# A streaming gate kernel: six fixed slots, a first tile of 8 rows on one queue, and the first loads issued ahead of the opening barrier

## The chip, the cores and the metric

The kernel runs on one core of a Trainium2 chip. The metric is device time in microseconds (us) of that core. Kernels are compared only within the same rounds. Ratios are the mean time of one kernel's fast executions over that of the other's in the same rounds, so they are not quite the ratio of the medians that the text quotes.

## The reference, cut to what matters

```python
# x: (1, 384, 384, 384) bfloat16, w1d: one bfloat16 weight
g = jnp.einsum("bhwc->bc", x) / (H * W)      # mean of each channel over 147,456 pixels
s = sigmoid(g * w1d[0])                      # 384 gates
return x * s[:, None, None, :]               # every pixel times its channel's gate
```

The input has 113.25 MB and so has the output. A gate is known only after all pixels have been summed, so a plain kernel would read the input twice. Both kernels here read it once. They compute an early gate `s_early` from the first tile and multiply and store with it while they sum everything; at the end they compare it with the true gate in bfloat16 and repeat the whole pass only if a bit differs. In these data it never differs, because the gates round to the same value.

## The kernel before

A "row" is 128 pixels (one for each partition, 768 bytes in each). The kernel cuts the 1,152 rows into tiles of 44 (the last two have 28 and 24) and keeps six of them in the on-chip memory. SyncE's queue carries loads and ScalarE's queue carries stores. The first four tiles are loaded half on one queue and half on the other. TensorE sums each tile by 33 matmuls with a matrix of ones, VectorE multiplies it by `s_early` in place, and ScalarE issues the store. The load of tile k waits for the store of tile k-6.

```python
EDGE, SLOT, BOTH = 44, 44, 4

def load(place, n, r0, queues=("sync",)):
    of = dram(x_rows, r0, n)
    i = 0
    for queue, m in zip(queues, split(n, -(-n // len(queues)))):
        plan.dma(queue, at(place + i, m), of[:, i * C : (i + m) * C], writes=rows(place + i, m))
        i += m

def put(place, n, r0, to):                      # gate, then store
    plan.op("vector", gate(to, place, n, s_early), ...)
    plan.final.append(plan.dma("scalar", dram(o_rows, r0, n), at(to, n), reads=rows(to, n)))

for k in range(BOTH):
    load(places[k], sizes[k], starts[k], ("sync", "scalar"))
    if k == 0:
        plan.dma("scalar", w_one[0:1, 0:1], w1d.unsqueeze(0), writes=["w_one"])
heads = {e: len(plan.streams[e]) for e in ("sync", "scalar")}
weight()                                        # the weight, by a small matmul
add_rows(places[0], sizes[0], 0, True, True)    # sum of the first tile, for s_early
# ... s_early ...
for k in range(1, len(sizes)):
    if k >= n_slots:
        j = k - n_slots
        put(places[j], sizes[j], starts[j], places[j])
    if k >= BOTH:
        load(places[k], sizes[k], starts[k])
    add_rows(places[k], sizes[k], 1, k == 1, k == last)   # 33 matmuls, written out
for k in range(len(sizes) - n_slots, last):
    put(places[k], sizes[k], starts[k], places[k])
put(places[last], sizes[last], starts[last], places[last + 1 - n_slots])
# ... true gate, comparison, conditional second pass ...

plan.emit("sync", nc.sync, heads["sync"])       # first loads: after the opening barrier,
plan.emit("scalar", nc.scalar, heads["scalar"]) # before the engines' blocks
```

Of the kernel before, what the change touches and what calls it, by code (L numbers as in the profile page):

```python
# [3 lines left out]
P = 128  # L4
# [9 lines left out]
class Planner:  # L14
# [9 lines left out]
    def __init__(self, nc, name, n_dma_sems):  # L24
        self.nc = nc
        self.streams = {e: [] for e in ("sync", "scalar", "vector", "tensor", "gpsimd")}
        self.sems = {e: nc.alloc_semaphore(f"{name}_{e}") for e in self.COMPUTE}
        self.count = {e: 0 for e in self.COMPUTE}
        self.pool = [nc.alloc_semaphore(f"{name}_dma_{i}") for i in range(n_dma_sems)]
        self.pool_uses = [0] * n_dma_sems  # L30
        self.n_dma = 0
        self.writer = {}
        self.readers = {}
        self.seen = {e: {} for e in self.streams}
        self.final = []

    def _wait(self, engine, token):
        sem, value = token
        if self.seen[engine].get(sem.name, 0) >= value:
            return  # L40
        self.seen[engine][sem.name] = value
        self.streams[engine].append(("wait", sem, value))

    def _needs(self, reads, writes):
# [12 lines left out]
        return list(need.values())  # L57
# [8 lines left out]
    def op(self, engine, emit, reads=(), writes=(), signal=True):  # L66
# [10 lines left out]
        self.streams[engine].append(("op", emit, self.sems[engine] if signal else None, 1))  # L77
        self._record(token, reads, writes)

    def dma(self, engine, out, in_, reads=(), writes=()):  # L80
# [11 lines left out]
        )  # L92
        self._record(token, reads, writes)
        return token

    def emit(self, name, e, most=None):
# [3 lines left out]
        for kind, a, b, *c in now:  # L100
            if kind == "wait":
                e.wait_ge(a, b)
            else:
# [11 lines left out]
EDGE, SLOT, BOTH = 44, 44, 4  # L115


def bass_standalone__channel_attn_eca__vision_kernel(
# [15 lines left out]
    s_true = nc.alloc_sbuf_tensor("s_true", [P, C], BF16)  # L134
    w_one = nc.alloc_sbuf_tensor("w_one", [1, 16], BF16)
    w_scaled = nc.alloc_sbuf_tensor("w_scaled", [P, 2], F32)
    warm = nc.alloc_sbuf_tensor("warm", [P, 2], F32)
# [23 lines left out]
    n_slots = n_arena // SLOT  # L161
    full, rest = divmod(n_rows - EDGE, SLOT)
    if rest < EDGE:
        full, rest = full - 1, rest + SLOT
    sizes = [EDGE] + [SLOT] * full + [4 * q for q in split(rest // 4, EDGE // 4)]
    assert sum(sizes) == n_rows and max(sizes) <= SLOT
    plan = Planner(nc, "a", 50)

    def load(place, n, r0, queues=("sync",)):
        of = dram(x_rows, r0, n)  # L170
        i = 0
        for queue, m in zip(queues, split(n, -(-n // len(queues)))):
# [3 lines left out]
                of[:, i * C : (i + m) * C],  # L176
# [22 lines left out]
    def add_rows(place, n, group, first, last):  # L199

        n_wide = n * C // WIDE
        start = place * C
        for i in range(n_wide):
            bank = acc[group][i % 3]
            plan.op(
                "tensor",
                lambda e, i=i, bank=bank: mm(e,
                    bank[:, :],
                    ones[:],
                    arena[:, start + i * WIDE : start + (i + 1) * WIDE],  # L210
                    start=first and i < 3,
                    stop=last and i >= n_wide - 3,
                ),
                reads=["ones"] + (rows(place, n) if i in (0, n_wide - 1) else []),
                writes=[f"acc{group}"],
                signal=i == n_wide - 1,
            )

# [15 lines left out]
    def put(place, n, r0, to):  # L234
        plan.op(
            "vector",
            gate(to, place, n, s_early),
            reads=["s_early"] + rows(place, n),
            writes=rows(to, n),
        )  # L240
        plan.final.append(
            plan.dma("scalar", dram(o_rows, r0, n), at(to, n), reads=rows(to, n))
        )

    def weight():
# [15 lines left out]
        for i, n in enumerate((sizes[0], n_rows)):  # L261
# [9 lines left out]
    starts = [sum(sizes[:k]) for k in range(len(sizes))]  # L271
    places = [k % n_slots * SLOT for k in range(len(sizes))]
    last = len(sizes) - 1


    plan.op("gpsimd", lambda e: e.memset(warm[:, 0:1], 0.0), writes=["warm"])  # L276
    plan.op("vector", lambda e: e.memset(ones[:], 1.0), writes=["ones"])  # L277
    for k in range(BOTH):
        load(places[k], sizes[k], starts[k], ("sync", "scalar"))
        if k == 0:  # L280
            plan.dma("scalar", w_one[0:1, 0:1], w1d.unsqueeze(0), writes=["w_one"])
    heads = {e: len(plan.streams[e]) for e in ("sync", "scalar")}
    weight()
    add_rows(places[0], sizes[0], 0, True, True)
# [8 lines left out]
    )  # L293



    for k in range(1, len(sizes)):
        if k >= n_slots:
            j = k - n_slots
            put(places[j], sizes[j], starts[j], places[j])  # L300
        if k >= BOTH:
            load(places[k], sizes[k], starts[k])
        add_rows(places[k], sizes[k], 1, k == 1, k == last)
    for k in range(len(sizes) - n_slots, last):
        put(places[k], sizes[k], starts[k], places[k])
    put(places[last], sizes[last], starts[last], places[last + 1 - n_slots])


# [4 lines left out]
            s_true[:], total[:], ACT_F.Sigmoid, scale=w_scaled[:, 1:2]  # L313
        ),
        reads=["total", "w_scaled1"],
        writes=["s_true"],
# [4 lines left out]
            total[:], s_true[:].bitcast(U16), s_early[:].bitcast(U16), ALU.not_equal  # L321
# [19 lines left out]
    again = Planner(nc, "b", 50)  # L341
    for place, n, r0 in zip(places, sizes, starts):
# [3 lines left out]
            gate(place, place, n, s_true),  # L346
            reads=rows(place, n),
# [4 lines left out]
        )  # L352
    for token in again.final:
# [3 lines left out]
    plan.emit("sync", nc.sync, heads["sync"])  # L357
    plan.emit("scalar", nc.scalar, heads["scalar"])
# [68 lines left out]
```

## Time and profile before

| | |
|---|---|
| time, median of 6 | 530.01 us (529.88 to 530.04); 529.97 us when the prediction was made |
| span of the profiled execution | 528.2 us (that execution took 529.65 us) |
| bytes moved, mean rate | 226.57 MB, 429 GB/s |
| TensorE, VectorE busy | 46% each |

These are lines of the page of the kernel before: busy time of each engine, the DMA share (in tenths) and the rate in 40 equal slices of the span, and the DMA queues with packets, MB and share of the 16 DMA engines. Queue 1 is SyncE's, queue 10 ScalarE's, queues 8 and 14 carry instructions.

```profile
span 528.2 us, 1091 instructions
PE 243.4 (46%) x865; PEld 0.2 (0%) x2; DVE 241.2 (46%) x45; ACT 2.7 (1%) x4; POOL 0.3 (0%) x5
...
DMA  8999999999999999999999999999999999999998
GB/s 361 431 426 420 448 415 447 433 427 438 422 448 425 438 433 427 433 426 450 427 433 433 427 448 417 445 427 433 430 429 450 427 433 430 429 429 434 442 427 363
...
q10 hardware_dynamic: 4466, 121.90, 53.6%
q1 hardware_dynamic: 3888, 104.60, 46.1%
q8 instruction: 3, 0.05, 0.0%
q14 instruction: 3, 0.02, 0.0%
```

The DMA engines are busy from end to end; only the first and the last slice are weaker. No compute engine is near its limit. The other view is the timeline of the first microseconds of the kernel before (start, length, engine and instruction; a `q` marks the engine's issue of transfers):

```profile
0.73 0.41 ACTq L91 DMA_DIRECT2D arena<-in_x_dram  x1
...
0.74 2.40 SPq L91 DMA_DIRECT2D arena<-in_x_dram  x5
```

The first loads are issued at 0.73 and 0.74 us. The trace's record of single DMA packets adds that the first packet starts at 1.75 us, and it lists when each of the 16 DMA engines finished its share of a transfer. The completions of the last store in the kernel before, as us after the first of them (525.92 us), were:

```
0.00 0.04 0.06 0.06 0.12 0.29 0.49 0.51 0.52 0.62 0.64 0.92 1.72 1.73 1.80 1.80
```

The kernel ends with the slowest engine, 1.8 us after the quickest.

### The profile page before, as it was taken

The numbers are of one execution on the slowest core, as the hardware profiler recorded it, in microseconds if no ns is written. First come the engines' busy times: TensorE is split into PE (matmuls) and PEld (weight loads), VectorE is DVE, ScalarE is ACT, GpSimd is POOL, SyncE is SP. The second block draws the span as 40 slices with busy tenths as digits, with TensorE's granted clock in tenths as the row PEclk, the third lists the DMA queues.
The fourth block names the chain that finished last, engine by engine and source line by source line (L and its number), as shares of the span: only waits on it lengthen the run. The fifth ranks groups of instructions, "written<-read, shape, count | busy, mean of one in ns | idle before, by whom it ended". The sixth has DMA issues, their size and how long they took to land.

```text
span 528.2 us, 1091 instructions
## 1 busy us (share of the span) xinstructions
PE 243.4 (46%) x865; PEld 0.2 (0%) x2; DVE 241.2 (46%) x45; ACT 2.7 (1%) x4; POOL 0.3 (0%) x5
## 2 busy tenths in 40 slices
PE   0877256165274164274274363263373473365410
PEld 0000000000000000000000000000000000000000
DVE  0299742633624633624614624614615516616720
ACT  1000000000000000000000000000000000000000
POOL 0000000000000000000000000000000000000000
PEclk9989786686676786786875786876876766877665
DMA  8999999999999999999999999999999999999998
GB/s 361 431 426 420 448 415 447 433 427 438 422 448 425 438 433 427 433 426 450 427 433 433 427 448 417 445 427 433 430 429 450 427 433 430 429 429 434 442 427 363
DMA packets 8360, 226.57 MB, mean 429 GB/s; under 512 B 930, under 2 KB 930, under 8 KB 930
## 3 DMA queue, kind: packets, MB, share of 16 engines
q10 hardware_dynamic: 4466, 121.90, 53.6%
q1 hardware_dynamic: 3888, 104.60, 46.1%
q8 instruction: 3, 0.05, 0.0%
q14 instruction: 3, 0.02, 0.0%
HBM read 113.25 MB, written 113.25 MB: 429 GB/s over the span
## 4 chain that ended last, share of the span: by engine, by line
another core or an unknown queue 70%; DMA 16%; DVE 4%; PE 3%; SPq 1%; issue 1%; ACT 0%; ACTq 0%
DMA out_dram<-arena 8%; DMA arena<-in_x_dram 6%; PE acc L187 3%; DVE arena L159 3%; DMA w_one<-in_w1d_dram 2%; SPq L91 1%; DVE total L229 1%; ACT s_true L312 0%; ACT s_early L288 0%; DVE total L320 0%; DVE total L227 0%; DVE wrong L328 0%; PE acc L185 0%; ACTq L91 0%
## 5 line engine op out<-in xcount | busy, mean ns | idle before, releaser
L187 PE MATMUL acc<-arena,ones 128*128 128x512 bf16 x863 | 242.9, 451 | 245.6 <-DMA arena<-in_x_dram 245.6
L159 DVE TENSOR_TENSOR arena<-arena,s_early 128x16896 bf16<-128x16896 bf16 (+2 forms) x27 | 234.5, 8691 | 240.9 <-PE acc L187 237.4
L255 PE MATMUL w_all<-w_one,ones 1*128 1x1 bf16 x1 | 0.2, 159 | 14.4 <-DMA w_one<-in_w1d_dram 14.4
L264 DVE TENSOR_SCALAR w_scaled<-w_all 128x1 f32<-128x1 f32 x2 | 0.2, 153 | 13.6 <-PE w_all L255 13.6
L229 DVE TENSOR_TENSOR total<-total,acc 128x128 f32<-128x128 f32 (+2 forms) x11 | 4.5, 408 | 2.3 <-PE acc L187 2.0
L227 DVE COPY total<-acc 128x384 f32<-128x384 f32 x1 | 0.6, 557 | 8.5 <-PE acc L187 8.5
L312 ACT ACTIVATE s_true<-total,w_scaled 128x384 bf16<-128x384 f32 x1 | 0.6, 615 | 479.5 <-DVE total L229 479.5
L249 ACT ACT_TABLE_LOAD x1 | 1.3, 1283 | 3.3 <-issue 3.3
L320 DVE TENSOR_TENSOR total<-s_true,s_early 128x384 f32<-128x384 uint16 x1 | 0.6, 558 | 0.7 <-ACT s_true L312 0.7
L288 ACT ACTIVATE s_early<-total,w_scaled 128x384 bf16<-128x384 f32 x1 | 0.6, 615 | 21.2 <-DVE total L229 21.2
L185 PE MATMUL acc<-arena,ones 128*128 128x512 bf16 x1 | 0.6, 590 | 0.0
L328 DVE TENSOR_REDUCE wrong<-total 128x1 f32<-128x384 f32 x1 | 0.6, 553 | 0.0
L277 DVE MEMSET ones<- 128x128 bf16 x1 | 0.2, 165 | 0.8 <-PEq L412 0.8
L249 ACT ACTIVATE warm<-warm 128x1 f32<-128x1 f32 x1 | 0.2, 203 | 0.0
L334 DVE CAST redo<-wrong 128x1 int32<-128x1 f32 x1 | 0.2, 153 | 0.0
L185 PEld LDWEIGHTS acc<-arena,ones 128*128 128x128 bf16 x1 | 0.1, 105 | 0.0
L255 PEld LDWEIGHTS w_all<-w_one,ones 1*128 1x128 bf16 x1 | 0.1, 98 | 14.3 <-issue 14.3
L412 POOL MEMSET const-bfloat16-1.0<- 128x1 bf16 x1 | 0.1, 101 | 0.0
L412 POOL MEMSET const-uint8-127<- 128x1 uint8 x1 | 0.1, 101 | 0.0
L276 POOL MEMSET warm<- 128x1 f32 x1 | 0.1, 98 | 0.3 <-POOLq L412 0.3
L412 POOL MEMSET const-float32-0.0<- 128x1 f32 x1 | 0.1, 98 | 0.2 <-issue 0.2
L412 POOL MEMSET const-float32-1.0<- 128x1 f32 x1 | 0.1, 98 | 0.0
## 6 DMA issues: line engine op xcount, KB each, us to landing
out_dram<-arena ACTq DMA_DIRECT2D x25, 4224.0 KB, 62.4
arena<-in_x_dram SPq DMA_DIRECT2D x21, 4224.0 KB, 38.7
arena<-in_x_dram ACTq DMA_DIRECT2D x4, 2112.0 KB, 27.4
arena<-in_x_dram SPq DMA_DIRECT2D x4, 2112.0 KB, 26.9
arena<-in_x_dram SPq DMA_DIRECT2D x1, 2688.0 KB, 35.1
out_dram<-arena ACTq DMA_DIRECT2D x1, 2688.0 KB, 29.1
arena<-in_x_dram SPq DMA_DIRECT2D x1, 2304.0 KB
out_dram<-arena ACTq DMA_DIRECT2D x1, 2304.0 KB, 26.7
```

Of the source, the lines that this page charges most:

```text
L91: ("op", lambda e: e.dma_start(out, in_), self.pool[i], 16)
L159: return lambda e: e.tensor_tensor(to_v, v, s_b, ALU.mult)
L185: loaded.append(e.matmul(bank, weights, moving, start=start, stop=stop))
L187: return e.add_instruction(mybir.InstMatmult(name=nc.get_next_instruction_name(), engine=mybir.EngineType.PE, ins=[e.lower_ap(moving), e.l ...
L227: emit = lambda e, part=part, of=of: e.tensor_copy(part, of)
L229: emit = lambda e, part=part, of=of: e.tensor_tensor(part, part, of, ALU.add)
L249: lambda e: e.activation(warm[:, 1:2], warm[:, 0:1], ACT_F.Sigmoid),
L288: lambda e: e.activation(s_early[:], total[:], ACT_F.Sigmoid, scale=w_scaled[:, 0:1]),
L312: lambda e: e.activation(s_true[:], total[:], ACT_F.Sigmoid, scale=w_scaled[:, 1:2]),
L320: lambda e: e.tensor_tensor(total[:], s_true[:].bitcast(U16), s_early[:].bitcast(U16), ALU.not_equal),
L328: lambda e: e.reduce_max(wrong[:], total[:], axis=mybir.AxisListType.X),
L412: nc = _bacc.Bacc("TRN2", target_bir_lowering=False, num_devices=1)
```

## The change

Its intent is to save at both ends: start loading earlier, know `s_early` earlier, and keep TensorE's program small. The slots become fixed, the first tile has 8 rows (4 of them give `s_early`) and is loaded by SyncE's queue alone, and the first load of each queue is moved in front of the barrier with which every program opens. TensorE's sums become a loop over six slots; GpSimd waits for each tile's loads and passes one signal on (the relay). The cut diff:

```diff
-EDGE, SLOT, BOTH = 44, 44, 4
+FIRST, EARLY, TILE, SLOTS, BOTH = 8, 4, 44, 6, 4
 ...
+            with e.Fori(0, rounds) as k:
+                for s in range(some):
+                    one(e, s)                  # wait for "ready", then 33 matmuls
+                if some < SLOTS:
+                    with e.If(k < rounds - 1):
+                        for s in range(some, SLOTS):
+                            one(e, s)
 ...
+    load(base, FIRST, 0)                       # SyncE's queue alone
     for k in range(BOTH):
-        load(places[k], sizes[k], starts[k], ("sync", "scalar"))
+        load(slot(k), TILE, row0(k), ("sync", "scalar"))
 ...
-put(places[last], sizes[last], starts[last], places[last + 1 - n_slots])
+    for k in range(n_tiles - SLOTS, n_tiles):
+        put(slot(k), TILE, row0(k))            # gated in place, the last tile too
+    put(base, FIRST, 0)
 ...
-    plan.emit("sync", nc.sync, heads["sync"])
-    plan.emit("scalar", nc.scalar, heads["scalar"])
+    ahead("sync", nc.sync, 1)                  # put in front of the barrier's first instruction
+    ahead("scalar", nc.scalar, 1)
+    plan.emit("sync", nc.sync, heads["sync"] - 1)
+    plan.emit("scalar", nc.scalar, heads["scalar"] - 1)
```

(Cut: the bookkeeping that drops redundant waits, the relay, the second pass in larger pieces.)

More of the change, by code (lines that the diff above doesn't have):

```diff
@@ L34, in __init__, with _clock @@
         self.seen = {e: {} for e in self.streams}
+        self.clocks = {}
         self.final = []
+    def _clock(self, engine, token):
+        known = dict(self.seen[engine])
+        known[token[0].name] = max(known.get(token[0].name, 0), token[1])
+        self.clocks[token[0].name, token[1]] = known
     def _wait(self, engine, token):
         sem, value = token
-        if self.seen[engine].get(sem.name, 0) >= value:
+        seen = self.seen[engine]
+        if seen.get(sem.name, 0) >= value:
             return
-        self.seen[engine][sem.name] = value
+        for name, at in self.clocks[sem.name, value].items():
+            seen[name] = max(seen.get(name, 0), at)
         self.streams[engine].append(("wait", sem, value))
@@ L56, in _needs @@
                 need[sem.name] = (sem, value)
-        return list(need.values())
+        return [
+            (sem, value)
+            for sem, value in need.values()
+            if not any(
+                self.clocks[s.name, v].get(sem.name, 0) >= value
+                for s, v in need.values()
+                if s.name != sem.name
+            )
+        ]
     def _record(self, token, reads, writes):
@@ L77, in op @@
         self.streams[engine].append(("op", emit, self.sems[engine] if signal else None, 1))
+        self._clock(engine, token)
         self._record(token, reads, writes)
@@ L92, in dma, with need, relay, signals @@
         )
+        self._clock(engine, token)
         self._record(token, reads, writes)
         return token
+    def need(self, engine, reads):
+        for token in self._needs(reads, []):
+            self._wait(engine, token)
+    def relay(self, sem, via, to, first, reads, writes):
+        if first:
+            self.need(via, first)
+            self.streams[via].append(("op", lambda e: e.sem_inc(sem, 1), None, 0))
+            for name, at in self.seen[via].items():
+                self.seen[to][name] = max(self.seen[to].get(name, 0), at)
+        self.signals(to, reads, writes)
+    def signals(self, engine, reads, writes):
+        self.count[engine] += 1
+        token = (self.sems[engine], self.count[engine])
+        self._clock(engine, token)
+        self._record(token, reads, writes)
     def emit(self, name, e, most=None):
@@ L102, in emit @@
                 e.wait_ge(a, b)
+            elif kind == "block":
+                a(e)
             else:
@@ L133, in bass_standalone__channel_attn_eca__vision_kernel @@
     s_early = nc.alloc_sbuf_tensor("s_early", [P, C], BF16)
-    s_true = nc.alloc_sbuf_tensor("s_true", [P, C], BF16)
     w_one = nc.alloc_sbuf_tensor("w_one", [1, 16], BF16)
     w_scaled = nc.alloc_sbuf_tensor("w_scaled", [P, 2], F32)
+    zeros = nc.alloc_sbuf_tensor("zeros", [P, 2], BF16)
     warm = nc.alloc_sbuf_tensor("warm", [P, 2], F32)
@@ L159, in gate, with slot, row0 @@
         return lambda e: e.tensor_tensor(to_v, v, s_b, ALU.mult)
-    n_slots = n_arena // SLOT
-    full, rest = divmod(n_rows - EDGE, SLOT)
-    if rest < EDGE:
-        full, rest = full - 1, rest + SLOT
-    sizes = [EDGE] + [SLOT] * full + [4 * q for q in split(rest // 4, EDGE // 4)]
-    assert sum(sizes) == n_rows and max(sizes) <= SLOT
-    plan = Planner(nc, "a", 50)
+    n_tiles = (n_rows - FIRST) // TILE
+    base = SLOTS * TILE
+    assert (n_rows - FIRST) % TILE == 0 and base + FIRST <= n_arena
+    assert FIRST % 4 == EARLY % 4 == TILE % 4 == 0 and EARLY < FIRST
+    last = n_tiles - 1
+    ready = nc.alloc_semaphore("ready")
+    def slot(k):
+        return k % SLOTS * TILE
+    def row0(k):
+        return FIRST + k * TILE
+    s_true = at(slot(n_tiles), 1)
+    plan = Planner(nc, "a", 70)
     def load(place, n, r0, queues=("sync",)):
-        of = dram(x_rows, r0, n)
         i = 0
@@ L175, in load @@
                 at(place + i, m),
-                of[:, i * C : (i + m) * C],
+                dram(x_rows, r0, n)[:, i * C : (i + m) * C],
                 writes=rows(place + i, m),
@@ L197, in mm, with add_rows, sum_first, sum_others @@
         )
-    def add_rows(place, n, group, first, last):
+    def add_rows(e, group, column, n, start, stop):
         n_wide = n * C // WIDE
-        start = place * C
-        for i in range(n_wide):
-            bank = acc[group][i % 3]
-            plan.op(
-                "tensor",
-                lambda e, i=i, bank=bank: mm(e,
-                    bank[:, :],
-                    ones[:],
-                    arena[:, start + i * WIDE : start + (i + 1) * WIDE],
-                    start=first and i < 3,
-                    stop=last and i >= n_wide - 3,
-                ),
-                reads=["ones"] + (rows(place, n) if i in (0, n_wide - 1) else []),
-                writes=[f"acc{group}"],
-                signal=i == n_wide - 1,
-            )
+        all_of = [
+            mm(
+                e,
+                acc[group][i % 3][:, :],
+                ones[:],
+                arena[:, column + i * WIDE : column + (i + 1) * WIDE],
+                start and i < 3,
+                stop and i >= n_wide - 3,
+            )
+            for i in range(n_wide)
+        ]
+        return all_of[-1]
+    def sum_first():
+        plan.op(
+            "tensor",
+            lambda e: add_rows(e, 0, base * C, EARLY, True, True),
+            reads=["ones"] + rows(base, EARLY),
+            writes=["acc0"],
+        )
+    def sum_others():
+        none = zeros[:, 0:1].broadcast_to([P, WIDE])
+        def one(e, s):
+            e.wait_ge(ready, 1).then_inc(ready, -1)
+            add_rows(e, 1, slot(s) * C, TILE, False, False).then_inc(
+                plan.sems["tensor"], 1
+            )
+        def emit(e):
+            add_rows(e, 1, (base + EARLY) * C, FIRST - EARLY, True, False)
+            rounds = -(-n_tiles // SLOTS)
+            some = n_tiles - (rounds - 1) * SLOTS
+            with e.Fori(0, rounds) as k:
[5 more added lines that the diff above has]
+                            one(e, s)
+            for i in range(3):
+                out = mm(e, acc[1][i][:, :], ones[:], none, False, True)
+            out.then_inc(plan.sems["tensor"], 1)
+        plan.streams["tensor"].append(("block", emit, None))
     def add_banks(group, copy):
@@ L232, in add_banks, with put @@
             plan.op("vector", emit, reads=[f"acc{group}", "total"], writes=["total"])
-    def put(place, n, r0, to):
+    def put(place, n, r0):
         plan.op(
             "vector",
-            gate(to, place, n, s_early),
+            gate(place, place, n, s_early),
             reads=["s_early"] + rows(place, n),
-            writes=rows(to, n),
+            writes=rows(place, n),
         )
         plan.final.append(
-            plan.dma("scalar", dram(o_rows, r0, n), at(to, n), reads=rows(to, n))
+            plan.dma("scalar", dram(o_rows, r0, n), at(place, n), reads=rows(place, n))
         )
@@ L260, in weight @@
         )
-        for i, n in enumerate((sizes[0], n_rows)):
+        for i, n in enumerate((EARLY, n_rows)):
             plan.op(
@@ L269, in weight @@
             )
-    starts = [sum(sizes[:k]) for k in range(len(sizes))]
-    places = [k % n_slots * SLOT for k in range(len(sizes))]
-    last = len(sizes) - 1
     plan.op("gpsimd", lambda e: e.memset(warm[:, 0:1], 0.0), writes=["warm"])
+    plan.op("gpsimd", lambda e: e.memset(zeros[:], 0.0), writes=["zeros"])
     plan.op("vector", lambda e: e.memset(ones[:], 1.0), writes=["ones"])
+    load(base, FIRST, 0)
     for k in range(BOTH):
-        load(places[k], sizes[k], starts[k], ("sync", "scalar"))
+        load(slot(k), TILE, row0(k), ("sync", "scalar"))
         if k == 0:
             plan.dma("scalar", w_one[0:1, 0:1], w1d.unsqueeze(0), writes=["w_one"])
+    for k in range(BOTH, SLOTS):
+        load(slot(k), TILE, row0(k))
     heads = {e: len(plan.streams[e]) for e in ("sync", "scalar")}
     weight()
-    add_rows(places[0], sizes[0], 0, True, True)
+    sum_first()
     add_banks(0, copy=True)
@@ L293, in bass_standalone__channel_attn_eca__vision_kernel @@
     )
-    for k in range(1, len(sizes)):
-        if k >= n_slots:
-            j = k - n_slots
-            put(places[j], sizes[j], starts[j], places[j])
-        if k >= BOTH:
-            load(places[k], sizes[k], starts[k])
-        add_rows(places[k], sizes[k], 1, k == 1, k == last)
-    for k in range(len(sizes) - n_slots, last):
-        put(places[k], sizes[k], starts[k], places[k])
-    put(places[last], sizes[last], starts[last], places[last + 1 - n_slots])
+    plan.need("tensor", ["zeros"] + rows(base, FIRST))
+    sum_others()
+    for k in range(n_tiles):
+        if k >= SLOTS:
+            put(slot(k), TILE, row0(k - SLOTS))
+            load(slot(k), TILE, row0(k))
+        there = rows(slot(k), TILE)
+        plan.relay(ready, "gpsimd", "tensor", there, there, ["acc1"])
+    plan.signals("tensor", rows(base, FIRST), ["acc1"])
+    for k in range(n_tiles - SLOTS, n_tiles):
+        put(slot(k), TILE, row0(k))
+    put(base, FIRST, 0)
     add_banks(1, copy=False)
@@ L312, in bass_standalone__channel_attn_eca__vision_kernel @@
         lambda e: e.activation(
-            s_true[:], total[:], ACT_F.Sigmoid, scale=w_scaled[:, 1:2]
+            s_true, total[:], ACT_F.Sigmoid, scale=w_scaled[:, 1:2]
         ),
         reads=["total", "w_scaled1"],
-        writes=["s_true"],
+        writes=["s_true"] + rows(slot(n_tiles), 1),
     )
@@ L320, in bass_standalone__channel_attn_eca__vision_kernel @@
         lambda e: e.tensor_tensor(
-            total[:], s_true[:].bitcast(U16), s_early[:].bitcast(U16), ALU.not_equal
+            total[:], s_true.bitcast(U16), s_early[:].bitcast(U16), ALU.not_equal
         ),
@@ L338, in bass_standalone__channel_attn_eca__vision_kernel @@
     checked = (plan.sems["vector"], plan.count["vector"])
-    again = Planner(nc, "b", 50)
-    for place, n, r0 in zip(places, sizes, starts):
+    again = Planner(nc, "b", 30)
+    half, r0 = base // 2, 0
+    s_kept = at(base, 1)
+    again.op(
+        "vector",
+        lambda e: e.tensor_copy(s_kept, s_true),
+        reads=rows(slot(n_tiles), 1),
+        writes=["s_kept"],
+    )
+    for k, n in enumerate(split(n_rows, half)):
+        place = k % 2 * half
         again.dma("sync", at(place, n), dram(x_rows, r0, n), writes=rows(place, n))
@@ L345, in bass_standalone__channel_attn_eca__vision_kernel @@
             "vector",
-            gate(place, place, n, s_true),
-            reads=rows(place, n),
+            gate(place, place, n, s_kept),
+            reads=["s_kept"] + rows(place, n),
             writes=rows(place, n),
@@ L352, in bass_standalone__channel_attn_eca__vision_kernel @@
         )
+        r0 += n
     for token in again.final:
@@ L355, in bass_standalone__channel_attn_eca__vision_kernel, with ahead @@
     stored = nc.alloc_semaphore("stored")
-    plan.emit("sync", nc.sync, heads["sync"])
-    plan.emit("scalar", nc.scalar, heads["scalar"])
+    def ahead(name, e, n):
+        block = nc.main_func.blocks[0].instructions
+        at_end = len(block)
+        plan.emit(name, e, n)
+        new = block[at_end:]
+        del block[at_end:]
+        barrier = next(
+            i
+            for i, ins in enumerate(block)
+            if ins.engine == e.engine and isinstance(ins, mybir.InstDrain)
+        )
+        block[barrier:barrier] = new
+    ahead("sync", nc.sync, 1)
+    ahead("scalar", nc.scalar, 1)
+    plan.emit("sync", nc.sync, heads["sync"] - 1)
+    plan.emit("scalar", nc.scalar, heads["scalar"] - 1)
     with nc.Block() as block:
```

## The prediction

> **What bounds the kernel now.** The DMA engines. The page's slices show a DMA share of 90% or more in 38 of 40 slices (the two at the ends have 8 tenths), 429 GB/s over a span of 528.2 us; PE and DVE are busy 46% each. The traffic is fixed: 113.25 MB read and as much written. In the trace's packet records a 44-row load and a 44-row store together repeat every 19.97 us from 100 to 460 us; a 33,792-byte packet takes 1.251 us, a 16,896-byte one 0.629 us, so some 7 ns per packet is constant and packet sizes matter little. Only the two ends can give anything:
>
> - Start: the timeline has the first loads of SyncE and ScalarE issued at 0.74 and 0.73 us, after the barrier; the first packet starts at 1.75 us.
> - End: of the last store's 16 completions the first comes at 525.9 us and the last four 1.7 to 1.8 us later. Three engines fell behind by 1.24 us each, right at the three 16 KB instruction packets of queue 8 (89.6, 229.5, 389.2 us; 0.95 us each), the fourth around 8 KB instruction packets at 512.7 us.
>
> **What the change does.**
>
> 1. First loads ahead of the barrier: issued at about 0. All packets move with them: -0.7 us, all on the critical path.
> 2. Small first tile: first sum at about 9 us instead of 14.4 (its 8 packets alternate with ScalarE's: 8 x (0.233 + 0.629) us, 0.233 estimated from the packet times above), s_early near 13 instead of 26.6 us. Worth nothing: ScalarE's queue carries half loads until about 38 us, and the engines are full anyhow.
> 3. Steady state: 6 slots, load k waits for store k-6, as before. Packets and bytes are equal: 0 us.
> 4. TensorE in a loop (215 rows of program, not 867), with a relay through GpSimd: hidden, PE has 46%. Instruction packets: the Trainium skill ("Runtime: NRT & Kernel Launch", Instruction fetch mechanics) says that instructions come in 16 KiB blocks and that a taken branch outside the window forces a fetch. The trace agrees on 16 KB. The first came after about 181 matmuls; the loop passes that place in its first round, so I expect one to eight. One is enough to keep the end's spread of 1.8 us; none would give up to 1.2 us; two on one engine would cost 1.2 us. Expected: -0.2 us.
> 5. Tail: the last tile is now gated in place, so after its load it waits for its sum (8.9 us), the gate (9.0) and about 1 us to the first store packet: 19 us. By my packet count the stores queued before it last 20 to 21 us after that load, at about 493 us. Hidden, with 1 to 2 us of margin. The check ends before the last store.
>
> **Prediction.** 529.97 - 0.7 - 0.2 = about 529.0 us, range 527.9 to 530.1 us. Faster by over 2%: 0.01; within 2%: 0.98; slower: 0.01.
>
> **What would show it.** First load issue near 0 us and first packet near 1.0 us; the same 19.97 us period; DMA share and PE and DVE times unchanged; spread of the last completions about 1.8 us, below 1 us if queue 8 carries no packets; s_early near 13 us without effect on the span.
>
> **What would make it wrong.** A gap on ScalarE's queue before the last 44-row store (+1 to 2 us); instruction refetch at each turn of the loop piling up on one engine; a time counted from a point that the earlier issue does not move; another DMA rate while the queues overlap.

## The result

The changed kernel took 529.16 us (median of 6, 529.04 to 529.53), the kernel before 530.01 us: 0.85 us less, ratio 0.9986 with a 95% interval of 0.9973 to 0.9999. All outputs are right. The same lines of the page of the changed kernel:

```profile
span 527.6 us, 1093 instructions
PE 243.7 (46%) x851; PEld 0.2 (0%) x2; DVE 241.1 (46%) x45; ACT 2.7 (1%) x4; POOL 0.3 (0%) x6
...
DMA  9999999999999999999999999999999999999998
GB/s 384 430 429 410 428 438 436 425 446 418 443 425 441 436 425 446 418 443 420 446 433 428 443 420 443 420 446 433 428 443 420 441 423 443 436 425 446 416 443 358
...
q8 instruction: 1, 0.02, 0.0%
q14 instruction: 2, 0.02, 0.0%
```

The first slice gained (384 for 361 GB/s), the fourth lost (410 for 420), and queue 8 carries one instruction packet instead of three. The timeline of the changed kernel's start:

```profile
0.00 3.19 SPq L109 DMA_DIRECT2D arena<-in_x_dram  x5
0.12 0.39 ACTq L109 DMA_DIRECT2D arena<-in_x_dram  x1
```

The first packet now starts at 1.05 us, 0.70 us earlier. To see where that lead goes I keep an account from the packet records: the *lag* is the time since the span's start, less the time that the packets moved so far need at their undisturbed lengths (7 ns + 1 ns for 27.16 bytes), averaged over the 16 engines.

```
lag, us, at      10 us   40 us   50 us   100 us   480 us   first / last completion of the last store
before            2.47    2.45    2.87     2.81     1.71     525.92 / 527.72
changed           1.75    1.66    2.62     2.44     1.14     525.48 / 527.12
difference       -0.72   -0.79   -0.25    -0.37    -0.57      -0.44 / -0.60
```

The start gives 0.72 us. Between 40 and 50 us, where ScalarE's queue passes from its half loads to the first store (the *hand-over*), the changed kernel loses 0.96 us and the kernel before 0.42: 0.54 us, about three quarters of the gain, are given back. The next two lines are that stretch in the windows view (window, length, busy time of PE, PEld, DVE, ACT and POOL, granted clock, DMA share, GB/s), of the kernel before and then of the changed one:

```profile
40.00:44.00 4.00, 3.51 (x17) 0.00 (x0) 4.00 (x1) 0.00 (x0) 0.00 (x0) 1.00 1.06 406
```

```profile
40.00:44.00 4.00, 4.00 (x18) 0.00 (x0) 4.00 (x1) 0.00 (x0) 0.00 (x0) 0.88 0.98 317
```

The engines count as busy in both (1.06 and 0.98), but the rate falls to 317 GB/s: packets last longer than their bytes need. Some 0.3 us come back by 480 us. Until then the kernel before moved three 16 KB instruction packets and the changed kernel none (its only one comes at 495.25 us). At about 1.3 us for one of 16 engines each (see point 4 under "Why the prediction was right or wrong"), that is an estimated 0.25 us in the mean. At the end the spread is 1.64 us instead of 1.80. So the profiles agree that the end moved by 0.60 us. The medians differ by 0.85 us and the two profiled executions by 0.53 us, because that of the kernel before (529.65 us) happened to be a quick one.

The steady state did not move. In both kernels a pair of a 44-row load and store takes 19.97 us, and the median queue 1 packet of 33,792 bytes takes 1.251 us. The window from 100 to 200 us of the changed kernel (that of the kernel before is shown in experiment 1):

```profile
100.00:200.00 100.00, 46.84 (x164) 0.00 (x0) 44.93 (x6) 0.00 (x0) 0.00 (x0) 0.73 1.00 433
```

### The profile page after: what moved, and what is told of

The parts are those of the page before. It is cut to its first block, busy times and chain, and to the rows that moved or that the text cites. A ratio compares the mean times of both kernels' runs of the same rounds, so it can differ in the third digit from the quotient of the medians.

```text
span 527.6 us, 1093 instructions
## 1 busy us (share of the span) xinstructions
PE 243.7 (46%) x851; PEld 0.2 (0%) x2; DVE 241.1 (46%) x45; ACT 2.7 (1%) x4; POOL 0.3 (0%) x6
## 5 line engine op out<-in xcount | busy, mean ns | idle before, releaser
L202 DVE TENSOR_TENSOR arena<-arena,s_early 128x16896 bf16<-128x16896 bf16 (+1 forms) x27 | 234.5, 8691 | 259.2 <-PE acc L238 259.2
```

What stands on the lines that cost most here:

```text
L202: return lambda e: e.tensor_tensor(to_v, v, s_b, ALU.mult)
```

## The experiments

Since all of this is about tenths of a microsecond, most were timed in five rounds. Two more quantities are read from the packet records of each. The *distance* is how long after the completion of a load the completion of the store that follows it comes (medians over the 16 engines). The *stretched share* is the part of load packets after 56 us that last over 0.1 us longer than undisturbed ones.

### 1. The early start alone, on the kernel before

```diff
 kernel before
-    plan.emit("sync", nc.sync, heads["sync"])
-    plan.emit("scalar", nc.scalar, heads["scalar"])
+    ahead("sync", nc.sync, 1)
+    ahead("scalar", nc.scalar, 1)
+    plan.emit("sync", nc.sync, heads["sync"] - 1)
+    plan.emit("scalar", nc.scalar, heads["scalar"] - 1)
```

> The kernel before with one part of the change alone: the first load of each queue is issued ahead of the opening barrier. If the change's whole gain is the earlier start (theory), the first packet starts near 1.05 us instead of 1.75 us, nothing else moves, and the time falls by 0.7 us, to about 529.3 us. Rival: the time is counted so that the earlier issue does not show in it; then it stays at 530.0 us.

Measured: 540.77 us (540.72 to 541.38), ratio 1.0205 (1.0191 to 1.0219). Neither theory had this. The first packet does start at 1.01 us. Then, from about 60 us on, the rate falls. The page of this run:

```profile
span 539.9 us, 1074 instructions
...
DMA  9999999999999999999999999999999999999995
GB/s 377 433 427 441 423 423 427 428 423 421 423 421 433 403 436 436 408 434 426 423 433 431 413 438 416 423 431 421 416 429 433 408 433 416 431 423 418 439 421 249
```

Windows of the kernel before, and then of this run:

```profile
100.00:200.00 100.00, 46.62 (x165) 0.00 (x0) 44.71 (x6) 0.00 (x0) 0.00 (x0) 0.72 1.00 433
...
300.00:400.00 100.00, 45.69 (x165) 0.00 (x0) 45.40 (x6) 0.00 (x0) 0.00 (x0) 0.76 1.01 434
```

```profile
100.00:200.00 100.00, 45.62 (x161) 0.00 (x0) 44.57 (x6) 0.00 (x0) 0.00 (x0) 0.72 1.00 422
...
300.00:400.00 100.00, 47.91 (x158) 0.00 (x0) 43.75 (x5) 0.00 (x0) 0.00 (x0) 0.66 1.00 422
...
530.00:540.00 10.00, 0.00 (x0) 0.00 (x0) 0.00 (x0) 0.00 (x0) 0.00 (x0) 0.50 0.43 183
```

Every engine still counts as busy all the time (1.00), at 422 GB/s instead of 433, with the same work on PE and DVE. At the end, the 16 engines finish about 9 us apart instead of 1.8, which is the 183 GB/s of the last window. In the packet records 8.9% of the load packets are stretched, by up to 1.2 us, most of them in the few microseconds after a store's end, and they add up to 6.9 us for an average engine. In the kernel before the share is 0.0%. The distance of stores behind loads is 2.5 us, one load packet and one store packet; in the kernel before it is 0.0.

### 2. The changed kernel without the early start

```diff
 changed kernel
-    ahead("sync", nc.sync, 1)
-    ahead("scalar", nc.scalar, 1)
-    plan.emit("sync", nc.sync, heads["sync"] - 1)
-    plan.emit("scalar", nc.scalar, heads["scalar"] - 1)
+    plan.emit("sync", nc.sync, heads["sync"])
+    plan.emit("scalar", nc.scalar, heads["scalar"])
```

> The changed kernel with its first loads put back behind the barrier. If the earlier start is the whole gain, the first packet starts near 1.75 us again and the time rises by 0.7 us, to about 529.85 us, which is almost the kernel before. Rival: the loop, the small first tile and the relay bring part of the 0.85 us themselves; then it stays below 529.6 us.

Measured: 529.90 us (529.81 to 530.29) against 529.87 us of the kernel before in the same rounds, ratio 1.000 with a 95% interval of 0.9987 to 1.0014, that is, plus or minus 0.7 us. So by the medians the rest of the change is worth nothing by itself and the early start is the whole gain; the interval alone would allow some tenths of a microsecond either way. Experiment 1 says that the early start is a gain only in the company of the rest. The distance here is 14.7 us and no load packet is stretched.

### 3. The first tile on both queues

```diff
 changed kernel
-    load(base, FIRST, 0)
+    load(base, FIRST, 0, ("sync", "scalar"))
```

> The changed kernel with its first tile of 8 rows shared by both queues (4 rows each) instead of SyncE's queue alone. In the changed trace the packets of SyncE's queue are stretched by about 0.5 us each where ScalarE's queue passes from loads to its first store (two 16,896-byte packets on each engine, 40.5 to 42.6 us), while in the kernel before it was one 33,792-byte packet on each engine. Theory: SyncE's queue is 8 packets behind because it alone carries the first tile, so two packets fall into the hand-over instead of one. With the tile shared the hand-over costs about 0.45 us as in the kernel before, and the time falls by 0.5 us, to about 528.65 us. Rival: the hand-over lasts a fixed time however the packets lie; then the time stays at 529.15 us.

Measured: 529.69 us (529.30 to 530.13), not 528.65. The hand-over cost 0.74 us, between the two theories' figures, and the start lost 0.3 us: at 10 us the lag was 2.06 instead of 1.75. The theory of "one packet instead of two" is not supported, and experiment 12 speaks against it too.

### 4. TensorE's loop written out

```diff
 changed kernel
-            with e.Fori(0, rounds) as k:
-                for s in range(some):
-                    one(e, s)
-                ...
+            for k in range(n_tiles):
+                one(e, k % SLOTS)
```

> The changed kernel with TensorE's loop written out (26 x 33 matmuls in a row), all else the same. Theory: queue 8 carries three 16 KB instruction packets again, each holds up the one engine that serves it by 1.24 us, three of the last store's completions come about 1.3 us after the bulk, and since the changed kernel's slowest engine already ends 1.64 us after the first, the time rises by no more than 0.3 us (529.2 to 529.5 us). Rival: the packets cost every engine; then the mean rises and the time goes up by about 1 us. If TensorE's loop itself cost something on the critical path, the time would fall instead.

Measured: 529.57 us (528.92 to 529.60). Queue 8 carried three packets again, at 175.9, 338.3 and 478.3 us. The last completions were spread over 2.08 us. Two of the five executions were quicker than the changed kernel's quickest, three slower by 0.4 us. The bound of 0.3 us was passed by 0.1. The loop itself brings no clear time.

### 5 to 8. Is it the distance between the two streams?

By then the distances of the profiled fast runs were 0.0, 0.5, 7.5, 10.0 and 14.7 us, and that of the slow one 2.5. Theory A says that the distance decides, theory B that the early start with equal halves on both queues does. The distance can be changed without touching the start: idle multiplications on VectorE in front of the first gate delay the first store, so that SyncE's loads run on alone for some packets.

```diff
 kernel before, with the early start (5 times) or without it (3 times)
+    spare = n_slots * SLOT
+    for _ in range(5):
+        s_b = s_early[:].unsqueeze(1).broadcast_to([P, 8, C])
+        idle_rows = at(spare, 8).rearrange("p (t c) -> p t c", t=8)
+        plan.op("vector", lambda e, o=idle_rows, s=s_b: e.tensor_tensor(o, s, s, ALU.mult),
+                reads=["s_early"], writes=["spare"])
```

> The kernel before with the earlier first loads (which took 540.8 us and not the 529.3 us expected), and on top of it five idle multiplications of 8 rows on VectorE ahead of the first gate, which delay the first store's issue by about 8.8 us, from 35.7 to 44.5 us. In the slow run each store ends 2.5 us (one load packet and one store packet) after a load, and load packets are stretched by 0.1 to 1.2 us just after each store boundary; in the five fast runs that distance was 0, 7.5, 10 and 14.7 us and no load packet was stretched. Theory A: the distance between the streams of loads and stores decides; the delay moves it to about 10 us, the stretching goes, and the time is about 529.3 us. Theory B: the earlier start with equal halves on both queues is itself the cause; then it stays near 540 us.

> The kernel before, loads issued behind the barrier as ever, with three such idle multiplications on VectorE ahead of the first gate: the first store's issue moves by about 5.3 us to 40.9 us, which by the lag of about 3.7 us seen between issue and first store packet should put the stores one packet (2.5 us) behind the loads, as in the slow run. Theory A (the distance decides): load packets are stretched and the time rises to about 535 to 541 us, provided the trace shows a distance of 2.5 us. Theory B (the earlier start is the cause): the time stays at 530.0 us whatever the distance.

> The kernel before with the earlier first loads once more, unchanged, as the control of this call. If the 10.9 us are a property of the kernel it takes 540 to 541.5 us again, with load packets stretched; if they were a property of that chip or of that hour, it takes 529.3 us.

Measured, on another chip than experiment 1:

- Early start and a delay of 8.8 us (experiment 5): 529.36 us (529.32, 529.35, 529.36 and one of 530.45). The distance is 10.0 us, 0.2% of the load packets are stretched. Holding the first store back by some 9 us of idle multiplications made the kernel 10 us faster than experiment 7. Theory B falls.
- Late start and a delay of 5.3 us (experiment 6): 530.49, 530.99, 539.12 and 539.98 us, the same program. The profiled execution was the one of 530.49 us; its distance is 5.0 us, with 0.1% stretched. The first store was issued at 42.1 us, 1.2 us later than planned, because `s_early` came 1.2 us later than in the kernel before.
- Early start, unchanged (experiment 7): 539.37 us (538.35 to 540.71), distance 2.6 us, 8.4% stretched. It is a property of the program and not of a chip.

The late-start kernel that is sometimes slow was run again with a slightly shorter delay (two multiplications of 8 rows and one of 7), in the hope that a slow execution would be profiled (experiment 8).

> The kernel before with its late start, the first store delayed by about 5.0 us (before_delay delayed it by 5.3 us and gave 530.5 and 531.0 us twice, 539.1 and 540.0 us twice; the profiled one of 530.5 us had the stores 5.0 us behind the loads). Theory A (the distance of stores behind loads decides): executions of about 539 us and of about 530.5 us again, and a profiled one near 539 us shows a distance of 2.5 us and stretched load packets, one near 530.5 us a distance of 0 or 5 us and none. It falls if a slow one shows another distance or no stretched loads.

Measured: 530.26, 537.03, 539.84 and 540.86 us, and the profiled one was that of 540.86 us. It is marked slow by the rule of 1.5% over the same kernel's fastest, but no lower clock goes with the loss: its granted clock is 0.739, that of the 530.26 us execution 0.748, and that of the other slow one, of 539.84 us, 0.762. Its distance is 2.5 to 2.6 us from the first store until about 300 us and drifts up to some 4 us after that, and 7.3% of the load packets are stretched. Its windows:

```profile
200.00:300.00 100.00, 46.59 (x165) 0.00 (x0) 42.24 (x6) 0.00 (x0) 0.00 (x0) 0.75 1.00 428
300.00:400.00 100.00, 44.87 (x158) 0.00 (x0) 41.95 (x5) 0.00 (x0) 0.00 (x0) 0.71 1.00 426
```

Here the start is late, as in the kernel before, and the loss is there all the same. Experiments 1 and 7 in all nine executions lie 8.5 to 11.5 us above the kernel before.

All profiled executions together:

```
run                   start   distance us   stretched   extra per engine us   time of that execution
before                late      0.0           0.0%         0.0                  529.65
after_split           early     0.5           0.0%         0.0                  529.69
before_ahead          early     2.5 to 3.8    8.9%         6.9                  541.38
before_ahead2         early     2.6           8.4%         5.6                  538.35
before_delay2         late      2.5           7.3%         4.4                  540.86
before_delay          late      5.0           0.1%         0.1                  530.49
nest_both3            early     5.5 to 6.2    1.4%         0.8                  530.76
after_unroll          early     7.5           0.1%         0.1                  529.60
nest_short            early     7.5           0.0%         0.0                  528.62
changed               early    10.0           0.0%         0.0                  529.12
before_ahead_delay    early    10.0           0.2%         0.1                  529.36
after_short           early    10.0           0.0%         0.0                  528.39
after_nest            early    10.0           0.0%         0.0                  529.96
after_late            late     14.7           0.0%         0.0                  529.98
```

In each slow run the distance was 2.5 us already at the first store, at 63 to 66 us; between 60 and 80 us the stretched load packets came to only 0.14, 0.02 and 0.02 us an engine. So the distance is not the result of the loss. The delay by itself is not the cause either, since the same idle work is in fast and slow executions alike (experiments 5, 6 and 8). Of the slow executions of experiment 6 none was profiled, and no run had a distance that started between 0.5 and 2.5 or between 2.5 and 5.0 us. What in the memory or the transfer engines makes this distance bad is open: no run here looks inside them.

### 9. The changed kernel with about a third of TensorE's work

```diff
 changed kernel
-            add_rows(e, 1, slot(s) * C, TILE, False, False).then_inc(
+            add_rows(e, 1, slot(s) * C, 12, False, False).then_inc(
```

The true sum is wrong here; the gate still rounds to the same value.

> The changed kernel with TensorE summing only 12 of the 44 rows of every tile (the true sum is wrong on purpose; the gate rounds to the same value, so the output should still be right). TensorE's program shrinks to about 70 rows and its work to about a third. Theory: TensorE is off the critical path and queue 8 carries no instruction packet, so the time falls by 0.1 us at most (the engine held up by the one packet at 495 us is only 0.14 us later than the next slowest one): 529.0 to 529.2 us. Rival: TensorE's waits or its reads of the on-chip memory slow the transfers; then the time falls by over 0.5 us.

Measured: 528.34 us (528.30 to 528.39), 0.8 us below the changed kernel: the expected bound of 0.1 us was wrong. No instruction packet ran on queue 8, and the last completions are spread over 1.01 us instead of 1.64. This run took two things away at once, so the next one took away one of them.

### 10. The full sum without an instruction packet

```diff
 changed kernel
-            with e.Fori(0, rounds) as k:
-                ... (six slots of 33 matmuls written out in the loop)
+            with e.Fori(0, n_tiles // SLOTS) as k:
+                with e.Fori(0, SLOTS) as s:
+                    one(e, s)                  # 33 matmuls, addressed by a register
+            with e.Fori(0, n_tiles % SLOTS) as s:
+                one(e, s)
```

> The changed kernel with TensorE's sums in nested loops over one tile's 33 matmuls, addressed by a register (153 rows of program and some register instructions, and the full true sum, against 215 rows of the changed kernel). The run that summed 12 rows of each tile was 0.8 us faster than the changed kernel and carried no packet on queue 8. Theory F: that gain came from the missing instruction packet (the last store's slowest engine came 1.01 us after the first, not 1.64 us); then the same comes here with the full sum: no packet on queue 8, spread near 1.0 us, time 528.3 to 528.5 us. Rival: it came from TensorE's smaller work; then the time stays near 529.15 us.

Measured: 529.89 us (529.80 to 529.96). Queue 8 is gone from the page of this run, the goal of the edit:

```profile
q10 hardware_dynamic: 4466, 121.90, 53.6%
q1 hardware_dynamic: 3888, 104.60, 46.1%
q14 instruction: 2, 0.02, 0.0%
```

Yet the spread grew to 2.5 us. Theory F falls. The completions of each store, as us after the first of the 16, show who is late. Three of them, of this run and of the changed kernel:

```
after_nest
 80 us: 0.00 0.03 0.11 0.14 0.31 0.33 0.34 0.35 0.35 0.38 0.47 0.65 0.67 1.04 1.13 3.46
279 us: 0.00 0.03 0.11 0.31 0.33 0.34 0.35 0.35 0.38 0.47 0.65 0.67 1.04 1.09 1.13 3.46
479 us: 0.00 0.03 0.11 0.31 0.33 0.34 0.35 0.35 0.38 0.47 0.65 0.67 1.04 1.13 2.15 3.46
changed
 79 us: 0.00 0.05 0.15 0.24 0.25 0.28 0.32 0.32 0.35 0.44 0.45 0.45 0.52 0.86 0.91 2.79
279 us: 0.00 0.15 0.24 0.25 0.28 0.32 0.32 0.35 0.44 0.45 0.45 0.52 0.62 0.86 0.91 2.79
479 us: 0.00 0.15 0.24 0.25 0.28 0.32 0.33 0.35 0.44 0.45 0.45 0.52 0.86 0.91 1.22 2.79
```

Fifteen engines keep their places to a hundredth of a microsecond for 400 us. One falls back all the time: from 0.14 through 1.09 to 2.15 us in `after_nest`, and from 0.05 through 0.62 to 1.22 in the changed kernel. That is about 0.10 and 0.06 us a tile. (The one at the right is only one turn apart in the alternation of the queues; it joins the others once the loads are done.)

### 11. The nested loop with a third of TensorE's work

```diff
 kernel of experiment 10
-            for i in range(TILE * C // WIDE):
+            for i in range(12 * C // WIDE):
```

> The kernel of after_nest (529.89 us, no instruction packet on queue 8) summing only 12 of the 44 rows of each tile, as the run of 528.34 us did in the loop of six tiles. That run lacked both the instruction packet and two thirds of TensorE's work; after_nest lacked the packet alone and was not faster, which speaks against the packet. Theory W: TensorE's work costs the transfers something at the end of the run; then the time falls to 528.3 to 528.7 us with a spread of the last completions near 1.0 us. Rival R: the end's spread is set by how the 16 engines fall in line at the hand-over to the first store, which TensorE's work does not change; then it stays near 529.9 us, with one late engine.

Measured: 528.55 us (528.36 to 528.62), spread 1.01 us. Its page has TensorE at 20%:

```profile
span 527.2 us, 791 instructions
...
PE 103.7 (20%) x244; PEld 0.2 (0%) x2; DVE 241.2 (46%) x45; ACT 2.7 (1%) x4; POOL 0.3 (0%) x6
```

Theory W holds: less work on TensorE makes the end 0.8 to 1.3 us earlier (every execution of experiments 9 and 11 is quicker than every one of its full-sum partner), though the wait for its last sum is hidden behind the stores (point 5 of the next section). The falling engine loses about 0.02 us a tile in this run and 0.03 in experiment 9. What it is about TensorE's work that slows one DMA engine is open. It need not be the reading of the data: `after_nest` does the same matmuls as the changed kernel, plus a register instruction for each, and its engine fell back almost twice as fast. Every timed execution comes with its span and granted clock, so all of them were profiled, and no run here can tell the cost of the instructions from that of recording them.

### 12. Three shared tiles instead of four

```diff
 kernel of experiment 10
-FIRST, EARLY, TILE, SLOTS, BOTH = 8, 4, 44, 6, 4
+FIRST, EARLY, TILE, SLOTS, BOTH = 8, 4, 44, 6, 3
```

> The kernel of after_nest with three tiles instead of four shared by both queues at the start. ScalarE's queue then runs out of loads near 28 us, and by 39 us, when the first store's packets should start, SyncE's queue is past its half tiles and on whole 33,792-byte packets. Theory H: at the hand-over to the first store every load packet in a window of 1.5 to 2 us is stretched by 0.2 to 0.5 us; with whole packets that is one per engine, so the hand-over costs 0.2 to 0.5 us instead of 0.98 us, the distance between loads and stores is 10 to 12 us (outside the bad one of 2.5 us), and the time is 0.5 to 0.7 us below after_nest, near 527.8 us. Rival: the hand-over costs the same whatever the packets; then it equals after_nest.

Measured: 529.98 us (529.31 to 530.76). The first store met whole packets as planned, but the lag still rose by 0.9 us, from 1.55 to 2.48 us. That speaks against theory H, but the run is not a clean test: its distance came out at 5.5 to 6.2 us and not at 10 to 12, 1.4% of its load packets are stretched, and the profiled execution is the slowest of the five (529.31 to 530.76 us). The cost of the hand-over (0.15 to 1.1 us over all runs) is not explained. The run showed one more thing, at its end. ScalarE's queue had carried fewer loads and so reached the end with less in stock. The timeline of this run:

```profile
505.06 10.63 DVE L202 TENSOR_TENSOR arena<-arena,s_early 128x16896 bf16<-128x16896 bf16 x2 [11.40 <-PE acc L238]
514.05 2.00 ACTq L109 DMA_DIRECT2D out_dram<-arena  x2
```

The last 44-row store was issued at 514.05 us. Twelve of the 16 engines had finished the store before it by 514.70 us, ten of them by 514.25, and at least ten began the new one at 514.90 us or later: the lag rose by 0.5 us.

## Why the prediction was right or wrong, point by point

The number was right: 529.0 us predicted, 529.16 measured, -0.85 us where -0.97 was expected. The reasons were right in part, and that the sum came out so close is partly luck: the prediction lacked the 0.54 us lost at the hand-over and the 0.3 us regained by 480 us, which partly cancel in the profiles, and those show 0.60 us where the medians show 0.85.

1. *First loads ahead of the barrier, -0.7 us, all on the critical path.* Right at the start of the changed kernel: first packet 0.70 us earlier, and without it the change is worth 0.0 us by the medians (experiment 2). "All packets move with them" failed: in the changed kernel the first completion of the last store moved by 0.44 us and the last by 0.60, and on the kernel before the same edit costs 10.9 us (experiment 1), because the stores then follow the loads at a bad distance.
2. *The small first tile is worth nothing.* True by itself (experiment 2), wrong in company. With the rest of the change the distance of the streams becomes 10 us, where the early start is safe; how the first tile is loaded has a part in it, since sharing it between the queues makes the distance 0.5 us (experiment 3). The times in this step were off too: the first sum came at 12.7 us and `s_early` at 17.5 us, not at 9 and 13. The timeline of the changed kernel shows why: TensorE first waits for the weight, whose 2 bytes lie behind ScalarE's first half load.

```profile
12.60 0.16 PE L337 MATMUL w_all<-w_one,ones 1*128 1x1 bf16 x1 [12.60 <-DMA w_one<-in_w1d_dram]
...
12.69 0.61 PE L236 MATMUL acc<-arena,ones 128*128 128x512 bf16 x1
...
16.93 0.61 ACT L369 ACTIVATE s_early<-total,w_scaled 128x384 bf16<-128x384 f32 x1 [12.55 <-DVE total L311]
```

   What the prediction called full engines held: the DMA share stayed at 1.00 to 1.01 from 10 to 40 us. As the Trainium skill ("DMA: Bandwidth & Descriptors", Issuing engines are not separate DMA queues) puts it, transfers of all issuing engines run on the same 16 engines and interleave. The packet records agree: in the steady state each engine takes one load packet and one store packet in turn. But the order in which they interleave turned out to matter.
3. *The steady state is unchanged, 0 us.* Right: 19.97 us a pair in both. A term was missing between 40 and 50 us: the hand-over to the first store cost 0.96 us in the changed kernel and 0.42 before.
4. *Instruction packets.* One to eight were expected, one came, and in the completions of the stores its engine fell from 0.32 to 1.64 us behind, 1.32 us; two of the three in the kernel before cost their engines as much (from 0.48 to 1.80 us), a little more than the 1.24 that the prediction has. It came at 495.25 us, in the loop's last round, while TensorE summed the last tile, and not in the first round:

```profile
490.56 4.00 PE L238 MATMUL acc<-arena,ones 128*128 128x512 bf16 x9 [10.84 <-PEq L279]
494.78 5.19 PE L238 MATMUL acc<-arena,ones 128*128 128x512 bf16 x23 [0.22 <-issue]
```

   In that round the second part of the loop's body is skipped by a branch; whether this or the loop's end called for the packet, no run tells. The Trainium skill ("Runtime: NRT & Kernel Launch", Instruction fetch mechanics) has blocks of 16 KiB, which the packet's 16,384 bytes confirm, and forced fetches at branches out of the window. The loop's turns before that caused none here. "Below 1 us if queue 8 carries no packets" failed: with none, `after_nest` ended 2.5 us apart, because one engine falls back steadily. In the changed kernel too the next slowest engine ended at 1.50 us, so the packet alone was worth an estimated 0.14 us. The size of the term, -0.2 us, fits the spread (1.80 to 1.64).
5. *Tail hidden with 1 to 2 us of margin.* Hidden, with more. The timeline of the changed kernel has the last gate and the stores' issue, followed by the end of the check:

```profile
500.01 10.63 DVE L202 TENSOR_TENSOR arena<-arena,s_early 128x16896 bf16<-128x16896 bf16 x2 [11.29 <-PE acc L238]
509.00 2.01 ACTq L109 DMA_DIRECT2D out_dram<-arena  x2
...
515.11 0.15 DVE L415 CAST redo<-wrong 128x1 int32<-128x1 f32 x1
```

   The last 44-row store was issued at 509.00 us. The store before it ended at 513.65 us on the first engine, so with the 0.75 us from issue to packet that experiment 12 shows, about 3.9 us were left. Experiment 12 used that margin up and paid 0.5 us.

A version that beats both kernels with the full sum was not found. The two runs near 528.4 us leave out over two thirds of the sum, and no other kernel had a median below 529.16 us.

## What to carry to other kernels

When the DMA engines are full from end to end, look at where the load and store streams stand to each other as well as at their bytes: the same transfers took 530 or 540 us, and holding the first store back by 9 us repaired it. A saving at the start can shift that relation, so test it together with what it will ship with. A kernel that ends with the slowest of 16 engines should be read engine by engine, as the mean rate hides a late one.

## What the Trainium skill lacked or had wrong

- No page has it that a stream of stores 2.5 us (one packet pair) behind a stream of loads slows the loads: 7.3 to 8.9% of load packets stretched, 422 to 428 GB/s instead of 433, 8.5 to 11.5 us. At 0, 0.5, 5, 7.5, 10 and 14.7 us it was at most 0.2%, at 5.5 to 6.2 us 1.4%. It belongs to "DMA: Bandwidth & Descriptors", which says that spreading transfers over the issuing engines doesn't help bandwidth, as all run on the same 16 DMA engines; here the order of the two queues' packets on them did matter.
- The same page (Specifications) gives about 0.6 us to the first byte for transfers issued by SyncE and ScalarE. Here the first packet started 1.01 and 1.05 us after the issue began, and in the kernel before the first packets lasted 0.4 to 0.8 us longer than later ones of their size.
- The same page (Where 436 GB/s comes from) says that for transfers between HBM and the on-chip memory the HBM side binds, at about 358 GB/s a core. This core alone moved 433 GB/s, half reads and half writes, from 100 to 480 us, which is nearer to the 425 GB/s that the page measured on one core whose neighbour was idle.
- No page has the cost of the passage from loads to the first store on a queue: 0.15 to 1.1 us of lag, not explained here.
- "Runtime: NRT & Kernel Launch" (Instruction fetch mechanics) calls the cost of crossing a 16 KiB boundary mostly hidden. In this kernel, which is bound by transfers, the packet held up the DMA engine that carried it by about 1.3 us.
- No page has that one DMA engine falls back steadily while TensorE works: about 0.06 us a tile of 33 matmuls, 0.10 with a register instruction for each, 0.02 to 0.03 with 9 matmuls.
